# An RWKV time mixer and an MLP mixer on one core: PSUM banks by order of release, one product moved to ScalarE, one chunk in another style, and a new order of all tasks

## The chip, the cores and the metric

The kernel runs on one core of a Trainium2 chip. A core has five engines with a queue of their own each: TensorE (PE), which multiplies matrices, VectorE (DVE), ScalarE (ACT), GpSimd (POOL) and SyncE (SP), which here issues transfers. Each takes its instructions strictly in the order in which they were written and waits on semaphores for the others. TensorE writes its results to PSUM, a memory of eight banks, from which VectorE and ScalarE take them. Transfers between the chip's main memory (HBM) and the on-chip SBUF run on 16 DMA engines. The metric is the device time in microseconds (us).

## The reference

The inputs r, k and v are [4, 8, 768, 48] (batch, heads, steps, head size) in f32, w and u are [8, 48]. First comes a recurrence over the steps, with one 48x48 state for each batch and head:

```python
for t in range(S):
    cur = einsum('bhd,bhe->bhde', u[None] * kt, vt)
    y[:, :, t] = einsum('bhd,bhde->bhe', rt, state + cur)
    state = w[None, :, :, None] * state + einsum('bhd,bhe->bhde', kt, vt)
```

With the heads put side by side y is x, [4, 768, 384]. It goes through a mixer over the steps and one over the channels, with weights [768, 256], [256, 768], [384, 1536] and [1536, 384]:

```python
h = maximum(xt @ w_tok1, 0) @ w_tok2        # xt is x with steps and channels exchanged
u = x + h.transpose(0, 2, 1)
out = u + maximum(u @ w_ch1, 0) @ w_ch2
```

## The kernel before

**The recurrence by chunks.** The 768 steps of a batch are six chunks of 128; there are 24 units (batch b, chunk c), numbered n = 6b + c. `unit` (it starts at `n = b * C + c`) writes the tasks of one. Powers of the decay w are multiplied into k (`kp`, which lies with its r partner in one of four tiles `kr`) and into r; both are transposed so that the head size lies on the partitions (`rk`); `scores` multiplies them (TensorE, `at_ps`, two banks for the even and odd heads); `masked` multiplies that with a mask of earlier steps (VectorE, `AT`); `outputs` multiplies with v, adds the state's part (`y_ps`), and `result` adds the own step's part `yd` (`x_b`). `add_state` gathers k times v in a bank for three chunks (`kv_ps`), and `keep_state` copies it; at the end of three chunks it is multiplied with `wGm`, a decay mask, on VectorE. `copy_v` casts v to bf16 (`vb`, ScalarE), and `own` makes `yd` on GpSimd from `vb` and the per-head sums `adg`.

The list `style` says how a unit's r and k are turned and how its `adg` is made:

- 'f32': TensorE transposes r unscaled in f32 (`trr`) and k scaled (`trk`), VectorE multiplies the decay into r as it takes it (`evac_r`); GpSimd makes `m` = k times r, TensorE transposes it (`mT_ps`) and multiplies with u (`ad_ps`). Two copies on ScalarE (`copy_m`, `copy_ad`) and one of the keys (`evac_k`) belong to it.
- 'pe': GpSimd or VectorE scales both (`mul_k`, `mul_r`), TensorE transposes them in one go (`turn_all`, `tr_ps`), ScalarE copies (`evac`). For `adg` GpSimd makes `ku` (`mul_u`), VectorE `rku` (`mul_rku`) and a sum over each head (`sum_rku`).
- 'dma': as 'pe', but a transposing DMA that SP issues (`turn_rk`) makes `rk`.

**The mixers.** `mixer` writes the tasks of one batch: `hidden` and `relu_h` (token mixing, `h1_ps`, named h_ps in the profile), `back` and `sum_u` (`hT_ps`, `u_sb`), then u transposed in two halves sg of three chunks each, on TensorE for batch 0 (`turn_pe`, `t_ps`, `copy_uT`) and by DMA for the others; `up` and `relu_z` for each of the 12 blocks jt of 128 hidden channels (`z_ps`, `zr`), `down` in three parts of four matmuls for each chunk (`h2_ps`, also h_ps in the profile), `sum_o` (`osb`) and a store.

**The order.** Nothing here is scheduled as the kernel is built: `add` files each task under a number, and `plan.run(ORDER)` calls the tasks in the order of a long list of numbers at the head of the file. The costs, ranks, `take` and `give` in the calls of `add` are read by nothing in the file. The list fixes the order within each engine's queue, and thereby which tasks wait for each other; the semaphores come from the tiles. 33 of the tasks are `keep_warm` fillers, matmuls on zeros that nobody reads, placed in the list like the others; 12 more stand at the start.

**PSUM.** Four banks serve the five tiles of the recurrence's core. The other four are a pool, `psM`, with `bufs=4` and the tag "m": each new tile takes the bank after that of the tile before, in rotation, and has to wait until what was last in that bank has been read. All mixers' tiles, all transposes and the fillers go through it.

**Loads.** SP issues 72 loads of 128 x 384 f32, from rows of 48 numbers, each of them a task of its own, and the stores and transposing DMAs between them. The weights are five DMAs on GpSimd's queue (`load_weights`: w_tok1, w_tok2, two halves of w_ch1, w_ch2), with a cast from f32 to bf16 on the way; `W_DEP` ties the issue of the fourth to the landing of k of batch 1, chunk 1, and that of the fifth to k of batch 1, chunk 2.

Of the kernel before, what the change touches and what calls it, by code (L numbers as in the profile page):

```python
# [21 lines left out]
class Plan:  # L22
# [17 lines left out]
    69, 71, 70, 72, 73, 74, 153, 1, 76, 146, 156, 12, 147, 0, 158, 165, 75, 13, 157, 14, 170, 154, 2, 15,  # L40
    160, 78, 148, 171, 174, 175, 3, 167, 77, 161, 4, 169, 177, 179, 79, 162, 168, 186, 163, 178, 181, 80,
    191, 5, 172, 195, 196, 200, 192, 81, 188, 202, 164, 198, 149, 182, 216, 6, 82, 190, 199, 203, 24, 207,
    189, 23, 166, 83, 25, 204, 212, 219, 183, 205, 217, 173, 220, 85, 209, 228, 7, 193, 206, 84, 211, 224,
    221, 208, 237, 225, 184, 88, 238, 226, 223, 185, 86, 240, 213, 249, 242, 187, 210, 227, 87, 233, 241,
    245, 229, 244, 234, 230, 89, 194, 263, 141, 246, 231, 254, 214, 90, 259, 232, 247, 255, 215, 42, 251,
    258, 248, 265, 235, 270, 253, 266, 142, 29, 261, 236, 267, 30, 95, 35, 262, 250, 252, 268, 143, 272,
    269, 256, 274, 277, 20, 26, 16, 257, 31, 589, 273, 271, 279, 275, 590, 276, 27, 280, 591, 19, 283, 40,
    592, 34, 593, 150, 28, 32, 17, 610, 594, 611, 606, 614, 595, 612, 94, 8, 33, 613, 615, 598, 22, 607,
    151, 93, 18, 46, 599, 286, 608, 38, 602, 91, 609, 287, 600, 291, 295, 596, 601, 21, 144, 105, 292, 616,
    44, 9, 43, 603, 617, 297, 47, 96, 152, 41, 642, 322, 650, 597, 644, 643, 315, 651, 646, 10, 645, 604,  # L50
    145, 652, 647, 316, 605, 648, 319, 278, 653, 49, 618, 649, 628, 323, 619, 624, 629, 11, 313, 284, 625,
    626, 285, 640, 314, 636, 627, 92, 664, 641, 637, 638, 665, 634, 296, 298, 639, 288, 635, 632, 301, 289,
    662, 633, 620, 290, 663, 302, 621, 622, 303, 660, 656, 623, 630, 661, 657, 306, 97, 631, 320, 308, 293,
    321, 658, 307, 102, 654, 391, 294, 659, 671, 99, 655, 324, 331, 333, 672, 100, 325, 666, 304, 326, 103,
    305, 667, 334, 309, 332, 311, 98, 310, 668, 337, 312, 104, 673, 669, 349, 338, 674, 101, 327, 329, 339,
    350, 328, 354, 670, 330, 352, 107, 676, 370, 356, 353, 106, 342, 371, 340, 357, 343, 375, 358, 345, 344,
    341, 109, 382, 373, 359, 346, 377, 389, 111, 361, 347, 360, 363, 374, 348, 362, 366, 110, 677, 365, 367,
    678, 364, 108, 397, 378, 390, 392, 384, 675, 679, 379, 402, 368, 112, 386, 380, 403, 385, 396, 691, 425,
    369, 381, 692, 395, 414, 383, 114, 387, 693, 398, 388, 116, 406, 696, 694, 695, 426, 408, 117, 429, 681,
    113, 697, 407, 409, 698, 682, 423, 699, 115, 701, 412, 683, 700, 413, 448, 442, 703, 702, 399, 704, 706,  # L60
    424, 680, 401, 419, 705, 707, 420, 440, 684, 431, 686, 400, 430, 415, 436, 443, 687, 441, 437, 404, 685,
    708, 446, 688, 120, 432, 709, 453, 405, 416, 457, 447, 689, 710, 418, 449, 711, 713, 417, 459, 690, 723,
    714, 712, 721, 724, 719, 722, 727, 126, 720, 715, 728, 476, 733, 716, 731, 118, 734, 725, 732, 735, 726,
    127, 433, 736, 421, 435, 729, 121, 454, 474, 434, 717, 730, 737, 422, 119, 718, 450, 508, 738, 438, 124,
    451, 766, 458, 452, 749, 123, 439, 767, 750, 460, 464, 768, 509, 475, 455, 463, 771, 477, 125, 465, 747,
    481, 512, 466, 757, 748, 480, 470, 772, 456, 758, 471, 769, 491, 773, 122, 753, 489, 774, 770, 745, 492,
    754, 775, 741, 746, 490, 131, 467, 742, 495, 751, 497, 132, 469, 761, 506, 752, 468, 762, 498, 484, 129,
    472, 507, 482, 486, 743, 128, 485, 739, 483, 744, 502, 473, 763, 740, 513, 503, 487, 764, 755, 531, 488,
    130, 759, 542, 756, 791, 765, 760, 496, 523, 525, 514, 786, 133, 792, 793, 515, 519, 787, 520, 540, 135,
    796, 798, 797, 794, 524, 788, 799, 134, 795, 516, 789, 801, 800, 536, 517, 805, 803, 537, 776, 802, 790,  # L70
    541, 777, 543, 140, 778, 559, 547, 781, 518, 548, 546, 782, 779, 549, 783, 804, 138, 553, 526, 499, 806,
    780, 808, 529, 530, 814, 809, 784, 812, 815, 501, 818, 807, 582, 500, 824, 813, 819, 820, 825, 822, 136,
    821, 550, 823, 576, 810, 551, 826, 785, 811, 552, 830, 137, 827, 828, 831, 504, 139, 829, 816, 505, 557,
    533, 817, 521, 534, 532, 866, 554, 522, 867, 574, 560, 868, 558, 832, 535, 565, 834, 869, 833, 836, 564,
    563, 835, 575, 538, 577, 837, 570, 848, 571, 870, 566, 846, 539, 581, 849, 861, 580, 847, 862, 583, 863,
    555, 864, 567, 556, 838, 865, 569, 856, 839, 568, 857, 584, 572, 585, 858, 573, 852, 859, 840, 853, 586,
    860, 844, 841, 850, 845, 587, 851, 842, 588, 854, 843, 886, 855, 881, 888, 887, 882, 896, 900, 897, 898,
    883, 901, 899, 889, 871, 884, 902, 890, 891, 872, 892, 885, 873, 893, 874, 876, 894, 875, 877, 895, 878,
    927, 929, 879, 928, 949, 930, 880, 941, 950, 931, 942, 945, 932, 947, 946, 903, 948, 921, 904, 925, 922,
    911, 926, 905, 912, 923, 906, 915, 924, 919, 916, 917, 920, 907, 918, 909, 908, 913, 910, 943, 914, 939,  # L80
    944, 961, 940, 956, 957, 951, 952, 953, 958, 954, 937, 955, 959, 933, 938, 960, 935, 934, 962, 936, 963,
    966, 967, 964, 968, 965, 976, 969, 977, 970, 971, 978, 972, 973, 979, 980, 974, 975,
# [4 lines left out]
def kernel(  # L87
# [29 lines left out]
    WARM = 3  # L117
    TR = 1.28
    STORE = ["SP"] * B
    RK = 4  # L120
    style = ['f32', 'f32', 'f32', 'f32', 'f32', 'f32', 'pe', 'pe', 'pe', 'pe', 'f32', 'f32', 'dma', 'dma', 'dma', 'dma', 'dma', 'dma', 'dma', 'dma', 'dma', 'dma', 'dma', 'dma']
    TURN_PE = {(0, c) for c in range(C)}
    DVE_KP = (0, 1, 2, 4, 7, 9,)
    W_AT = (19.5, 21.5, 23.5, 0.0, 0.0)
# [10 lines left out]
    psM = ctx.enter_context(tc.tile_pool(name="psM", bufs=4, space=bass.MemoryType.PSUM))  # L135
# [50 lines left out]

    def keep_warm(n):
        for _ in range(n):
            z_ps = psM.tile([128, 512], f32, name="idle_ps", tag="m")
            pe.matmul(z_ps, warm[:, 0:128], warm, start=True, stop=True)  # L190

# [38 lines left out]
    wd_ps = psM.tile([128, H], f32, name="wd_ps", tag="m")  # L230
# [19 lines left out]
    def decay_rT(g):  # L250
        if g == 0:
            for a in range(HP):
                act.activation(wpT[:, g, a, :], steps[:, ts(g, T)], Exp, scale=lnwd[:, a:a + 1])
        else:
            act.activation(wpT[:, g], wpT[:, g], Exp)
# [6 lines left out]
    for q in range(2):  # L262
        rows = slice(q * P, (q + 1) * P)
        act.activation(lnwd[rows, :], wd_ps[rows, q::2], Ln)
    decay_rT(0)
# [40 lines left out]
    exps = {g: setup("POOL", 1.05, lambda g=g: exponents(g), (-1, g), after=6.3) for g in (1, 2)}  # L306
    t_wn = {g: setup("ACT", 0.52, lambda g=g: decay_k(g), (0, g, 0)) for g in (1, 2)}
    t_wpT = {g: setup("ACT", 0.53, lambda g=g: decay_rT(g), (0, g, 0), [exps[g]]) for g in (1, 2)}

    def group_decay():  # L310
# [3 lines left out]
    t_wGm = setup("POOL", YD, lambda: pool.tensor_mul(  # L314
        wGm, bm, wG.unsqueeze(2).unsqueeze(3).to_broadcast([128, HP, 2, D])), (1, 0), [t_wG])
# [16 lines left out]
    for i, (n, c) in enumerate(((48, 0.0574), (16, 0.152), (24, 0.152), (24, 0.152), (96, 0.081))):  # L332
        t_w[i] = add("POOL", 0.85, lambda i=i: load_weights(i), rank=(-2, i), late=1.2, dma=(n, c), after=W_AT[i], deps=[t_load.get(W_DEP.get(i))])

    u_ps = {}

    def turn_u():
        u_ps["d"] = psM.tile([128, 3], f32, name="ud_ps", tag="m")
        pe.matmul(u_ps["d"], u_rows, ident_f[0:3, 0:3], start=True, stop=True)

    def block_u():
        dve.tensor_mul(u_blk, heads, u_ps["d"].unsqueeze(2).to_broadcast([128, 3, H]))

    def spread_u():
        u_ps["b"] = psM.tile([128, dm], f32, name="u_ps", tag="m")
        pe.matmul(u_ps["b"], ones, u_row, start=True, stop=True)

    def copy_u():
        act.copy(u_bc, u_ps["b"])

# [21 lines left out]
    def unit(b, c, prev):  # L372
# [36 lines left out]
        def turn(key, src, idt, dt):  # L409
            def f():  # L410
                L[key] = psM.tile([128, HP, T], dt, name=key, tag="m")
                for a in range(HP):
                    pe.transpose(L[key][:, a, :], pair(src(), a), idt)
            return f
# [6 lines left out]
        def turn_m():  # L421
            L["mT_ps"] = psM.tile([128, 3, T], f32, name="mT_ps", tag="m")
# [339 lines left out]
```

## Time and profile before

The seven runs of the kernel have a median of 174.89 us, from 173.38 to 176.16.

| what | us |
|---|---|
| the profiled execution's own time | 174.34 |
| its span, first to last instruction | 172.6 |
| TensorE busy | 163.9 |
| of that, fillers (`idle_ps`) | 14.9 |
| VectorE, ScalarE, GpSimd busy | 110.0, 91.8, 88.9 |
| TensorE's last matmul starts | 168.9 |
| last load issued by SP | 119.9 |

The span is what the page's rows add up to; the 1.7 us between it and the execution's time lie outside the recorded instructions. In the page a row of 40 digits gives an engine's busy share, in tenths, in each fortieth of the span (4.3 us). A group row reads: line, engine, operation, what is written and from what, count, then busy time in all and nanoseconds of one, then the idle time ahead of these instructions and what ended it. Every line is L143, the helper that writes all instructions in program order, so the tiles' names tell the work apart. Rows in order of time give start, duration, engine, and in brackets an idle time and what ended it. TensorE's matmuls overlap in the pipeline, so that rows are longer than the distance of their starts: 0.49 us from one `up` task (three matmuls) to the next.

### The profile page before, as it was taken

How to read it: one execution, taken by the hardware profiler on the slowest of the kernel's cores; microseconds unless marked ns; L12 is line 12 of the kernel's file. 1: busy time of each engine (PE TensorE's matmuls, PEld its weight loads, DVE VectorE, ACT ScalarE, POOL GpSimd, SP SyncE). 2: the span in 40 equal slices, each digit the busy share in tenths (PEclk: the TensorE clock that was granted, in tenths of full speed). 3: DMA queues.
4: the chain of work that ended last, by engine and by line, in shares of the span. 5: the costliest groups of instructions: out<-in, count | busy, mean ns of one | idle time of the engine just before them, and what ended most of it. 6: DMA issues, size and time to landing. Idle time of an engine off the chain costs nothing.

```text
span 172.6 us, 3854 instructions
## 1 busy us (share of the span) xinstructions
PE 163.9 (95%) x1456; PEld 103.9 (60%) x1457; DVE 110.0 (64%) x197; ACT 91.8 (53%) x211; POOL 88.9 (51%) x108
## 2 busy tenths in 40 slices
PE   6999898999799999999999899999999999999992
PEld 2568785556466787656566466565666656566560
DVE  7577994868946979799289862993958154000321
ACT  2899560389798287131965574048552510992300
POOL 5459799079900977999844999514850000000000
PEclk9999999999999999999999999999999999999999
DMA  4999999999998599899999999999571108200222
GB/s 91 203 199 198 175 184 213 204 188 166 197 187 165 117 223 219 178 234 157 241 221 152 257 227 172 189 242 227 106 167 49 46 1 202 70 4 0 91 91 91
DMA packets 101722, 27.38 MB, mean 159 GB/s; under 512 B 95173, under 2 KB 101705, under 8 KB 101705
## 3 DMA queue, kind: packets, MB, share of 16 engines
q1 hardware_dynamic: 98112, 23.80, 73.6%
q0 software_dynamic: 3408, 3.15, 11.4%
q10 hardware_dynamic: 184, 0.20, 0.5%
q8 instruction: 11, 0.18, 0.4%
q14 instruction: 7, 0.05, 0.1%
HBM read 20.65 MB, written 4.72 MB: 147 GB/s over the span
## 4 chain that ended last, share of the span: by engine, by line
PE 54%; DMA 19%; SPq 11%; DVE 9%; POOL 2%; issue 2%; ACT 0%; POOLq 0%; DVEq 0%
PE h_ps L143 24%; PE z_ps L143 19%; SPq L143 11%; DMA kt<-in_k_dram 8%; DMA wch<-in_moe_w_ch_dram 5%; DMA wtok<-in_moe_w_tok_dram 4%; DVE u_sb L143 3%; PE y_ps L143 3%; PE hT_ps L143 3%; PE at_ps L143 2%; DVE rku L143 2%; DVE AT L143 2%; DMA vt<-in_v_dram 2%; POOL ku L143 1%; POOL yd L143 1%
## 5 line engine op out<-in xcount | busy, mean ns | idle before, releaser
L143 ACT ACTIVATE zr<-z_ps 128x384 bf16<-128x384 f32 x96 | 45.5, 493 | 30.8 <-PE z_ps L143 30.5
L143 PE MATMUL z_ps<-uT,wch 128*128 128x384 bf16 x288 | 51.1, 326 | 1.2 <-DMA wch<-in_moe_w_ch_dram 1.2
L143 PE MATMUL h_ps<-wch,zr 128*128 128x384 bf16 x288 | 52.2, 326 | 0.0
L143 DVE TENSOR_TENSOR AT<-at_ps,mask 128x512 bf16<-128x512 f32 x48 | 31.5, 684 | 13.2 <-PE at_ps L143 13.2
L143 PEld LDWEIGHTS <-wch 128*128 128x128 bf16 x288 | 27.0, 98 | 19.0 <-DMA wch<-in_moe_w_ch_dram 1.5
L143 PEld LDWEIGHTS <-zr 128*128 128x128 bf16 x288 | 27.3, 98 | 16.8
L143 POOL TENSOR_TENSOR yd<-vb,adg 128x384 f32<-128x384 bf16 x24 | 20.8, 868 | 21.2 <-ACT vb L143 9.9
L143 DVE TENSOR_TENSOR osb<-u_sb,h_ps 128x384 f32<-128x384 bf16 x24 | 13.2, 550 | 24.4 <-PE h_ps L143 24.3
L143 DVE TENSOR_TENSOR rku<-ku,rt 128x384 f32<-128x384 f32 x16 | 19.9, 1248 | 2.7 <-POOL ku L143 2.4
L143 POOL TENSOR_TENSOR ku<-kt,u_bc 128x384 f32<-128x384 f32 x16 | 16.7, 1050 | 7.5 <-DMA kt<-in_k_dram 7.4
L143 POOL TENSOR_TENSOR kr<-kt,wn 128x384 bf16<-128x384 f32 x18 | 18.7, 1037 | 0.0
L143 POOL TENSOR_TENSOR kr<-rt,wp 128x384 bf16<-128x384 f32 x16 | 16.9, 1058 | 3.4 <-DMA rt<-in_r_dram 3.3
L143 DVE TENSOR_TENSOR u_sb<-x_b,hT_ps 128x384 bf16<-128x384 bf16 x24 | 12.3, 545 | 9.1 <-PE hT_ps L143 9.1
L143 ACT CAST vb<-vt 128x384 bf16<-128x384 f32 x24 | 12.3, 511 | 10.6 <-DMA vt<-in_v_dram 10.4
L143 DVE TENSOR_TENSOR x_b<-y_ps,yd 128x384 bf16<-128x384 f32 x24 | 13.2, 551 | 5.9 <-PE y_ps L143 5.0
L143 PE MATMUL idle_ps<-warm 128*128 128x512 bf16 x44 | 14.9, 432 | 1.7 <-DVE warm L143 1.5
L143 PEld LDWEIGHTS <-rk 48*128 48x128 bf16 (+1 forms) x272 | 10.2, 95 | 7.9 <-issue 5.6
L143 ACT CAST S<-kv_ps 48x192 bf16<-48x192 f32 x32 | 10.0, 312 | 6.7 <-PE kv_ps L143 5.2
L143 PEld LDWEIGHTS <-wtok 128*128 128x128 bf16 x96 | 8.8, 98 | 7.3 <-DMA wtok<-in_moe_w_tok_dram 1.2
L143 PEld LDWEIGHTS <-kr 128*128 128x128 bf16 x144 | 9.3, 99 | 3.8 <-issue 0.9
L143 PE MATMUL hT_ps<-h1r,wtok 128*128 128x384 bf16 x48 | 10.3, 326 | 0.1
L143 POOL TENSOR_TENSOR m<-kt,rpad 128x384 f32<-128x384 f32 x8 | 8.5, 1066 | 2.9 <-PE kv_ps L143 1.8
(72 smaller groups left out, 159.0 us busy)
## 6 DMA issues: line engine op xcount, KB each, us to landing
kt<-in_k_dram SPq DMA_DIRECT2D x24, 192.0 KB, 4.1
vt<-in_v_dram SPq DMA_DIRECT2D x24, 192.0 KB, 4.3
out_dram<-osb SPq DMA_DIRECT2D x24, 192.0 KB, 2.6
rt<-in_r_dram SPq DMA_DIRECT2D x16, 192.0 KB, 3.8
rpad<-in_r_dram SPq DMA_DIRECT2D x8, 192.0 KB, 4.6
wch<-in_moe_w_ch_dram POOLq DMA_DIRECT2D x2, 576.0 KB, 9.0
wch<-in_moe_w_ch_dram POOLq DMA_DIRECT2D x1, 1152.0 KB, 13.9
wtok<-in_moe_w_tok_dram POOLq DMA_DIRECT2D x2, 384.0 KB, 7.1
```

The lines of the kernel that those rows point to most:

```text
L143: return lambda *args, **kw: tc.keep_in_program_order(f(*args, **kw))
```

## The change

Four things change in the code; the list `ORDER` is replaced.

1. PSUM banks: a small class hands out the four banks of `psM` from a list of free ones. A tile takes the bank that has been free longest; the task that reads the tile last gives the bank back at that place of the program. Each bank has a tag of its own with one buffer.
2. `wGm` is made by four ScalarE activations with a per-partition scale, no longer by one GpSimd product. (The tuple `EXPS` names the groups whose decay GpSimd prepares; it holds the same two groups as before.)
3. Unit 10 (batch 1, chunk 4) goes from style 'f32' to 'pe'. It has three tasks less, so the tasks' numbers after it shift.
4. The planning numbers of the weights change, which nothing in the file reads.

```diff
+    class Buffers:
+        def __init__(self, pool, tag, n):
+            self.pool, self.tag, self.free, self.held = pool, tag, list(range(n)), {}
+
+        def take(self, shape, dtype, name):
+            i = self.free.pop(0)
+            t = self.pool.tile(shape, dtype, name=name, tag=f"{self.tag}{i}", bufs=1)
+            self.held[id(t)] = (i, t)
+            return t
+
+        def give(self, t):
+            self.free.append(self.held.pop(id(t))[0])
+
+    banks = Buffers(psM, "m", 4)
...
-                L[key] = psM.tile([128, HP, T], dt, name=key, tag="m")
+                L[key] = banks.take([128, HP, T], dt, key)
...
             def evac_k():
                 act.copy(rk_tile()[:, 0], L["trk"])
+                banks.give(L["trk"])
...
-    t_wGm = setup("POOL", YD, lambda: pool.tensor_mul(
-        wGm, bm, wG.unsqueeze(2).unsqueeze(3).to_broadcast([128, HP, 2, D])), (1, 0), [t_wG])
+    def group_mask():
+        for a in range(HP):
+            act.activation(wGm[:, a], bm[:, a], ACTF.Copy, scale=wG[:, a:a + 1])
+
+    t_wGm = setup("ACT", 0.75, group_mask, (1, 0), [t_wG])
...
-    style = [... 'pe', 'pe', 'pe', 'pe', 'f32', 'f32', 'dma', ...]
+    style = [... 'pe', 'pe', 'pe', 'pe', 'pe', 'f32', 'dma', ...]
```

All other tiles of `psM` are taken and given back in the same manner. Of the new order, this is what the prediction speaks of. The number of fillers is the same. On GpSimd, w_tok1 is issued behind five `m`, one `kp` and two `yd` (before: five `m`, one `kp`, four `yd` and `wGm`), and between the fourth and fifth weights stand `ku`, `kp`, `yd`, `ku`, `mul_r` (before: two `ku`). On SP, v of batch 0, chunk 2 is the 16th issue (before: the 10th), r of batch 0, chunk 1 the 9th (before: the 5th), and r and k of batch 1, chunk 4 the 28th and 27th (before: the 33rd and 32nd). On ScalarE the cast of v of batch 1, chunk 0 stands ahead of the first mixer's relu (before: behind it and the first `copy_uT`). On TensorE the units of batches 1 to 3 stand ahead of more of the mixers' `up` and `down` tasks than before, and nine fillers lie between the last `hidden` of batch 0 and its first `up` (before: 16). On VectorE `rku` of batch 1, chunk 4 and that of chunk 2 stand ahead of the first `masked` of batch 1, and that of chunk 3 stands between the masks of chunks 0 and 1.

## Prediction

> **What bounds the kernel now.** I read the page's busy rows first, then the same rows by stage, then TensorE's own instructions in order of time, then the queues that feed it.
>
> ```profile
> PE 163.9 (95%) x1456; PEld 103.9 (60%) x1457; DVE 110.0 (64%) x197; ACT 91.8 (53%) x211; POOL 88.9 (51%) x108
> PE   6999898999799999999999899999999999999992
> ...
> PEclk9999999999999999999999999999999999999999
> ...
> L143 PE MATMUL idle_ps<-warm 128*128 128x512 bf16 x44 | 14.9, 432 | 1.7 <-DVE warm L143 1.5
> ```
>
> TensorE is busy nearly everywhere at full clock, but 14.9 us of that are fillers (`idle_ps`) that compute nothing. The stages, cut at the first channel-mixing matmul (`z_ps`), show where they lie:
>
> ```profile
> 0.00:38.60 38.60, 35.62 (x331) 23.29 (x333) 28.41 (x64) 22.75 (x58) 25.76 (x44) 1.00 1.08 184
> 38.60:45.60 7.00, 5.87 (x43) 3.55 (x41) 5.94 (x4) 6.62 (x15) 6.98 (x8) 1.00 1.13 180
> 45.60:130.00 84.40, 83.22 (x818) 53.50 (x819) 63.99 (x109) 46.48 (x106) 56.15 (x58) 1.00 1.06 192
> ```
>
> Before 38.60 TensorE waits for loads, units and weights and fills the time; after it, it works almost without a hole. In order of time:
>
> ```profile
> 37.72 1.04 PE L143 MATMUL idle_ps<-warm 128*128 128x512 bf16 x3
> 38.60 2.11 PE L143 MATMUL z_ps<-uT,wch 128*128 128x384 bf16 x12
> ...
> 45.63 0.66 PE L143 MATMUL z_ps<-uT,wch 128*128 128x384 bf16 x3 [1.16 <-DMA wch<-in_moe_w_ch_dram]
> ```
>
> Two holes more of this kind follow: 0.68 us before `kv_ps` at 77.96 and 0.47 us before `at_ps` at 99.23. So the span is the time of the first `z_ps` (38.6), the work behind it, 2.3 us of holes, and 3.4 us from TensorE's last matmul (169.2) to the end (one VectorE sum, 0.56, and a store). Whatever shortens the span must bring the first `z_ps` forward, take work from TensorE, or close holes; whatever opens new holes behind 38.6 costs its full length.
>
> **The change, part by part.** *Banks.* No instruction is added or removed. Where TensorE waited for a bank in this profile is read from the waits: 0.5 us (`mT_ps` for the copy of `adg`), 0.5 (`at_ps`, which the change doesn't touch) and 0.3 (weights for `zr`). So the new hand-out is worth between 0 and 0.8 us by itself; I take 0, because each bank is still waited for by the task that takes it, and the rest of its worth is in what order it allows.
>
> *Mask product to ScalarE.* GpSimd loses one `wGm` product, 0.83 us at 16.6, which stands ahead of the token weights' issue. ScalarE gets four products of 128x96. Near rows are the 48x192 cast, 312 ns, and the 128x8 copy, 164 ns, so 4 x 164 = 0.65 to 4 x 312 = 1.25 us. They stand behind the key copy of chunk 2; behind them wait `copy_ad` of chunk 2 and `copy_m` of chunk 1. ScalarE has 2.4 us of idle time between 16.4 and 20.0 (0.60, 0.47 and 1.33 us before three of its rows), so I cost it at 0; without that cover it would be up to 1.25 us on the first `z_ps`.
>
> *Chunk 10 (batch 1, chunk 4) as 'pe' in place of 'f32'.* From the chain of the last work, TensorE loses `trr` 0.44, `trk` 0.22, `mT_ps` 0.48 and `ad_ps` 0.62, and gains one `tr_ps` of eight transposes, 0.45: 1.3 us less. ScalarE swaps 0.59 + 0.49 + 0.16 for one copy of 1.01 us. GpSimd does `kr`, `kr`, `ku` for `kr`, `m`: 1.0 us more. VectorE swaps one `rk` product (0.68) for `rku` (0.84 in the middle of its rows) and a sum (0.55): 0.7 us more. GpSimd and VectorE have the room on average, not in every stretch (below).
>
> *The order, the front.* Before, GpSimd issues `wtok1` at 21.80, behind five m products, a kr product, four yd, the wGm and the two exponents. After, two yd and wGm stand behind the issue or are gone: 3 x 0.83 = 2.5 us less ahead of it, of which I take 2.0, since the m product of chunk 1 now waits for a load that is issued ninth and not fifth. So `wtok1` is issued at 19.8 and lands at 26.6 with the 6.8 us that it took. The value load of chunk 2 moves from the tenth to the sixteenth place in SP's queue, where this trace issues at 16.0 and loads land some 5 us later, at 21.0; its state and the work that is written behind it up to the first token matmul (4.4 us of TensorE) put that at 26.6 too, against 28.62. This gain is then eaten: behind it stand four fillers and the last chunk's output, whose mask product waits in VectorE's queue for a `rku` of the next batch. I get the last token matmul at 31.0 (30.86 before). From there to the first `z_ps` it is 7.7 us before, with 16 fillers; after, there are nine, sg0 comes first in place of sg1, and all six `t_ps` stand ahead. Six VectorE sums at 0.46 apart, the last behind one kr product, end at 36.6; the last transpose follows, two fillers, and `z_ps` starts at 37.3: 1.3 us earlier. The bounds are 36.3 (as the fillers count) and 38.6 (as before). The TensorE tasks ahead of it are also 0.3 us more, taken from behind.
>
> *The order, the weights.* They are GpSimd's own issues.
>
> ```profile
> 35.66 1.12 POOL L143 TENSOR_TENSOR yd<-vb,adg 128x384 f32<-128x384 bf16 x1 [5.79 <-DVE u_sb L143]
> 36.73 0.80 POOL L143 DMA_DIRECT2D wch<-in_moe_w_ch_dram  x1
> 37.55 1.97 POOL L143 TENSOR_TENSOR ku<-kt,u_bc 128x384 f32<-128x384 f32 x2
> 39.45 1.07 POOL L143 DMA_DIRECT2D wch<-in_moe_w_ch_dram  x1
> ```
>
> The second half of w_ch1 waits 5.79 us behind a yd; that is the 1.16 us hole at 45.63. The VectorE work named was done at 31.9; its last input is the cast `vb` on ScalarE, at 35.03, behind a `copy_uT`. After, this cast stands ahead of the mixer's first relu in ScalarE's queue, and the next limit is the key load of batch 1, chunk 1, which the issue is tied to: with loads landing some 2.8 us apart while weights move, about 33.5, and the issue at 34.5. With 8.85 us it lands at 43.4; its first use is at 43.1, so this hole closes, within what the estimate can tell. w_ch2 moves back: five GpSimd products stand between the two issues in place of two, and I get its issue at 42 for 39.45, since `ku` of chunk 4 waits for its key. Its 13.9 us shared the queue with the piece before (landed 7.8 us apart), so alone I estimate 10.5 to 13.9, landing 52.5 to 56; the first down matmul stands at 52.8 unstalled and 55 with the holes below. I take no hole, up to 1.5.
>
> *The order, the units behind.* TensorE's list asks for everything earlier. Counting its rows from 37.3, the mask inputs (`at_ps`) of batch 1, chunk 4 stand at 54.7 (before 64.55), the next batch's token matmuls at 63 (70.66), batch 2, chunk 4 at 87 (96.46), batch 3, chunk 5 at 122 (131.25). SP's queue at its present pace allows that: the last r/k turn is its 99th issue, and the 98th of this trace is at 119.9 with some 4 us of pauses. The narrow place is batch 1. The r load of chunk 4 lands near 42 by the loads moved, so its `rku` runs to 43.5; the next `rku`, two sums and two mask products (0.68 each) follow in VectorE's order, and the masks of chunk 0 end at 47.6 where TensorE wants the next `at_ps` at 46.3. A further `rku` does the same once more, 0.7. I take 2.0 us of holes there, and 1.15 later, as the two of this trace.
>
> Sum against the profiled execution (span 172.6, its time 174.34): -1.3 (chunk 10), -0.3, -1.3 (first `z_ps`), -2.3 (old holes), +3.2 (new ones) = -2.0, span 170.6. That execution lies 0.55 below the median of 174.89, so 174.9 - 2.0 = 172.9.
>
> **A rule against it.** `rku` has a row far off its group:
>
> ```profile
> 40.35 0.55 DVE L143 TENSOR_REDUCE adg<-rku 128x8 f32<-128x384 f32 x1
> 40.90 0.27 DVE L143 MEMSET kr<- 128x256 uint32 x1
> 41.09 6.43 DVE L143 TENSOR_TENSOR rku<-ku,rt 128x384 f32<-128x384 f32 x1
> ```
>
> GpSimd runs products back to back from 40.55 to 47.1, and `rku` ends 0.4 us behind them. The Trainium skill (SBUF — State Buffer, section "SBUF: two separate sides") says that a VectorE instruction with two SBUF inputs and a GpSimd one exclude each other for one whole instruction. By the rule as it reads, `rku` waits for one product, 1.0 us, and the holes stay at 3.2; by this row it waits for the whole run. It speaks against this change, which puts `rku` ahead of masks that TensorE waits for. Nine of 16 `rku` took under 0.9 us, six 0.95 to 1.35, so I hold to the short ones and make the long one a rival.
>
> **The rivals.** *The order holds (170.9).* If the batch-1 holes don't come, the sum has 1.15 in place of 3.2: -4.05. For it: the new holes rest on a landing that I estimate to within 2 us. Against: VectorE's queue has no slack there.
> *Weights late (174.4).* w_ch2 lands as late as it did after its issue: 1.5 us more, -0.5. For it: 13.9 is the row; against: it shared its queue.
> *VectorE shut out (176.7).* In batch 1, between 42 and 55, `rku` of chunks 4 and 3 wait to the end of GpSimd's runs of three to four products (45.0 and 52.1, when GpSimd itself comes to a product that needs their sums). The masks of chunk 0 and 1 then end at 48.6 and 55.0, where TensorE wants them at 46.5 and 49.9: 5.1 us of holes, 1.15 later and 0.8 for one more such case: 7.05 for 3.2, +1.8. From 5.2 us of holes on nothing is gained; from 6.9 it is over 1% slower.
>
> **How the numbers follow.** Chances: sum as worked 0.33, order holds 0.25, weights late 0.18, shut out 0.24. A measurement of this kernel tells about 1% (1.75 us) from no change. Below 173.1 lie the order case, over half of the likeliest and little of the late weights: 0.46. Above 176.6 lies some two thirds of the shut-out case and a tail of the others: 0.21. The rest, 0.33, is within 1%. The predicted time is the likeliest, 172.9 (its own range 171.5 to 174.3); the range of all runs from 170.4 to 177.4.
>
> **What would show it.** Right: first `z_ps` near 37.3 with fewer fillers just ahead; no wait on `wch` over 0.5 us at 43 to 45; holes on TensorE of about 2 us between 44 and 55, behind `AT`; `rku` under 1.4 us. Wrong: first `z_ps` at 38.6 or later (a yd, a load or a bank ahead of it), holes over 5 us behind the first `z_ps` (`AT`, `wch`, `kr`), or none at all.

## The result, and the profile after

The changed kernel takes 173.49 us (median of 24 runs), the kernel before 174.54 us in the runs that were taken with it (61 in all). The ratio is 0.9918, with a 95% interval from 0.9892 to 0.9943: 0.8% faster, about 1.4 us. Some executions of every kernel are disturbed, longer and mostly at a lower granted clock; all ratios and median spans below leave them out, and without them the changed kernel's median is 172.90. The profiled execution took 173.01 us, with a span of 171.0 (172.6 before).

The busy rows, the groups of the fillers and of `rku`, and the shares of the chain of work that ended last, from the page of the changed kernel:

```profile
PE 163.5 (96%) x1447; PEld 104.0 (61%) x1448; DVE 106.6 (62%) x198; ACT 91.1 (53%) x213; POOL 89.7 (52%) x108
...
PEclk9999999999999999999999999999999999999999
DMA  4999999999999999999999999899421146100222
...
PE 77%; DMA 12%; DVE 6%; ACT 1%; issue 1%; SPq 1%; ACTq 0%; DVEq 0%
...
L144 DVE TENSOR_TENSOR rku<-ku,rt 128x384 f32<-128x384 f32 x17 | 16.4, 963 | 3.1 <-POOL ku L144 2.0
L144 PE MATMUL idle_ps<-warm 128*128 128x512 bf16 x44 | 16.0, 452 | 1.6 <-DVE warm L144 1.5
```

TensorE is on the chain for 77% of the span (54% before), yet it still spends 16.0 us on fillers (14.9 before, of the same number). What it won was not won ahead of the first `z_ps`. The stages and TensorE's rows from there on:

```profile
0.00:38.86 38.86, 36.47 (x338) 24.62 (x340) 28.33 (x65) 24.73 (x65) 26.44 (x44) 1.00 1.10 181
38.86:45.60 6.74, 6.03 (x44) 3.69 (x43) 3.17 (x7) 5.26 (x14) 5.19 (x6) 1.00 1.05 203
45.60:130.00 84.40, 83.39 (x828) 53.11 (x826) 65.24 (x110) 47.58 (x108) 58.04 (x60) 1.00 0.99 190
```

```profile
38.86 2.11 PE L144 MATMUL z_ps<-uT,wch 128*128 128x384 bf16 x12
41.62 0.33 PE L144 MATMUL kv_ps<-vb,kr 128*128 128x96 bf16 x4 [0.65 <-ACT vb L144]
...
53.71 0.40 PE L144 MATMUL at_ps<-rk 48*128 48x128 bf16 x8 [1.01 <-DVE AT L144]
```

The first `z_ps` stands at 38.86, not earlier than the 38.60 before. Behind it there are two holes, 1.66 us in all, both in batch 1; the three of before (2.31 us) are gone, the wait for `wch` among them. The span divides as follows:

| us | before | after | difference |
|---|---|---|---|
| first `z_ps` | 38.60 | 38.86 | +0.26 |
| holes behind it | 2.31 | 1.66 | -0.65 |
| the rest behind it | 131.69 | 130.48 | -1.21 |
| span | 172.6 | 171.0 | -1.6 |

### The profile page after: what moved, and what is told of

Read it like the earlier page. It is cut to its first block, busy times and chain, and to the rows that moved or that the text cites. A ratio compares the mean times of both kernels' runs of the same rounds, so it can differ in the third digit from the quotient of the medians.

```text
span 171.0 us, 3824 instructions
## 1 busy us (share of the span) xinstructions
PE 163.5 (96%) x1447; PEld 104.0 (61%) x1448; DVE 106.6 (62%) x198; ACT 91.1 (53%) x213; POOL 89.7 (52%) x108
## 4 chain that ended last, share of the span: by engine, by line
PE 77%; DMA 12%; DVE 6%; ACT 1%; issue 1%; SPq 1%; ACTq 0%; DVEq 0%
PE h_ps L144 31%; PE z_ps L144 22%; DMA vt<-in_v_dram 6%; DMA rt<-in_r_dram 4%; PE y_ps L144 4%; PE at_ps L144 4%; PE hT_ps L144 4%; PE idle_ps L144 3%; DVE rku L144 2%; DMA wp<-in_w_dram 2%; PE trr L144 2%; PE kv_ps L144 2%; PE ad_ps L144 2%; DVE AT L144 1%; PE mT_ps L144 1%; DVE kr L144 1%
## 5 line engine op out<-in xcount | busy, mean ns | idle before, releaser
L144 PE MATMUL z_ps<-uT,wch 128*128 128x384 bf16 x288 | 52.0, 326 | 0.1
L144 PE MATMUL h_ps<-wch,zr 128*128 128x384 bf16 x288 | 51.6, 326 | 0.0
L144 PEld LDWEIGHTS <-wch 128*128 128x128 bf16 x288 | 26.6, 98 | 16.7 <-issue 0.2
L144 POOL TENSOR_TENSOR kr<-kt,wn 128x384 bf16<-128x384 f32 x18 | 19.5, 1085 | 3.2 <-DMA kt<-in_k_dram 1.4
L144 POOL TENSOR_TENSOR ku<-kt,u_bc 128x384 f32<-128x384 f32 x17 | 17.6, 1036 | 5.4 <-DMA kt<-in_k_dram 4.8
L144 POOL TENSOR_TENSOR kr<-rt,wp 128x384 bf16<-128x384 f32 x17 | 17.9, 1054 | 2.5 <-DMA rt<-in_r_dram 2.5
L144 DVE TENSOR_TENSOR rku<-ku,rt 128x384 f32<-128x384 f32 x17 | 16.4, 963 | 3.1 <-POOL ku L144 2.0
L144 PE MATMUL idle_ps<-warm 128*128 128x512 bf16 x44 | 16.0, 452 | 1.6 <-DVE warm L144 1.5
L144 PEld LDWEIGHTS <-kr 128*128 128x128 bf16 x148 | 10.1, 99 | 4.5 <-issue 1.4
L144 PE MATMUL at_ps<-rk 48*128 48x128 bf16 x192 | 9.6, 218 | 1.0 <-DVE AT L144 1.0
L144 PE MATMUL hT_ps<-h1r,wtok 128*128 128x384 bf16 x48 | 9.4, 326 | 0.1
```

Source lines behind the costliest of these rows:

```text
L144: return lambda *args, **kw: tc.keep_in_program_order(f(*args, **kw))
```

## The experiments

Ratios are to the kernel before on the same chip, with 95% intervals.

### The changed kernel once more

No edit.

> The changed kernel again, nothing edited, for a second trace. Two theories for its first up matmul (z_ps) at 38.86 us where 37.3 was predicted. Chance: TensorE's half pace up to 10.2 us in the first trace was one execution's; here transposes and fillers run at full pace from about 6 us, first scores stand at 10 to 11 us, z_ps near 37.4, span near 169.6. Order: the list itself makes it late (the last chunk's masks stand behind a rku and a sum of the next batch, and the first z_ps behind five sums): z_ps again at 38.5 to 39.2 and span 170.5 to 171.5, wherever the pace turns. Ratio to the kernel before 0.990 to 0.994 by either.

Measured: 172.24 us in the profile, ratio 0.9893 (0.9801 to 0.9985). TensorE's start was fast. Its rows, of the first trace and then of this one:

```profile
6.28 1.46 PE L144 MATMUL idle_ps<-warm 128*128 128x512 bf16 x3
```

```profile
6.11 0.82 PE L144 MATMUL idle_ps<-warm 128*128 128x512 bf16 x3
```

The same three fillers take 0.82 us in place of 1.46, and the `at_ps` of 19.57 in the first trace stands at 17.68 here. But that lead of 1.9 us is lost at once, in a wait for an `m` of GpSimd that the first trace does not have; the next `at_ps` stands at 22.32 for 22.61:

```profile
20.82 0.55 PE L144 MATMUL mT_ps<-ident_f,m 128*128 128x128 f32 x3 [1.43 <-POOL m L144]
```

So the first `z_ps` follows at 38.45: the two starts differ by 0.4 us there, and the other 1.15 to the predicted 37.3 are in the order or in the loads. The holes behind it are 1.58 us, though not the same ones:

```profile
44.14 0.40 PE L144 MATMUL tr_ps<-ident,kr 128*128 128x128 bf16 x4 [0.74 <-POOL kr L144]
53.02 0.40 PE L144 MATMUL at_ps<-rk 48*128 48x128 bf16 x8 [0.84 <-DVE AT L144]
```

The first hole waits here for GpSimd's scaled r of batch 1, chunk 0, which stands behind a `ku` that waited 2.13 us for k of chunk 4, and there for v of chunk 2: around 42 us TensorE runs into the loads, whichever comes last. The second recurs.

### Chunk 10 alone

```diff
-    style = [... 'pe', 'pe', 'pe', 'pe', 'f32', 'f32', 'dma', ...]
+    style = [... 'pe', 'pe', 'pe', 'pe', 'pe', 'f32', 'dma', ...]
```

in the kernel before; in its list 350 (`m`) becomes `mul_r`, `mul_u`, 352 (`trk`) becomes `turn_all`, 353 (`evac_k`) becomes `evac`, 356 (`evac_r`) becomes `mul_rku`, `sum_rku`, and the chunk's other 'f32' tasks go.

> The kernel before with chunk 10 (batch 1, chunk 4) alone turned to 'pe': banks in rotation, wGm on GpSimd, old list, the new tasks in the places of the old ones (mul_r and ku where m stood, rku and its sum where evac_r stood, the one turn where trk stood). The prediction's term: TensorE 1.3 us less work behind the first z_ps, so 173.0 for 174.3, ratio 0.9925. Rival: the two more GpSimd products (1.0 us) and the rku and sum (0.7 us on VectorE) come late in a list not made for them, and TensorE waits as much as it saves: ratio 0.998 to 1.004, with a new wait on kr, AT or tr_ps of 1 us or more between 55 and 70 us.

Measured: ratio 1.0019 (0.9969 to 1.0068); median span 172.7, that of the kernel before on this chip 172.7. The 1.3 us (0.9925) did not arrive. TensorE's rows of the stretch, then VectorE's:

```profile
63.62 0.33 PE L141 MATMUL y_ps<-S,rk 128*128 128x96 bf16 x4
64.06 0.20 PE L141 MATMUL y_ps<-vb,AT 128*128 128x48 bf16 x1
64.66 0.35 PE L141 MATMUL y_ps<-vb,AT 128*128 128x48 bf16 x7 [0.40 <-DVE AT L141]
64.94 0.40 PE L141 MATMUL at_ps<-rk 48*128 48x128 bf16 x8
```

```profile
61.88 0.93 DVE L141 TENSOR_TENSOR rku<-ku,rt 128x384 f32<-128x384 f32 x1
62.85 0.55 DVE L141 TENSOR_REDUCE adg<-rku 128x8 f32<-128x384 f32 x1
63.33 1.28 DVE L141 TENSOR_TENSOR AT<-at_ps,mask 128x512 bf16<-128x512 f32 x2
```

From the first `y_ps` row to the next `at_ps` it is 1.32 us; in the kernel before the same tasks take 0.46 (64.09 to 64.55). VectorE's new `rku` and sum stand ahead of the masks that these outputs wait for, and 0.86 us of the 1.3 go back at once. What is left is too little to be seen in the time; in this one trace the part behind the first `z_ps` is, without its holes, 131.05 us for 131.69. So what TensorE saved counted here only for what the list did not make it wait for VectorE again.

### Banks in rotation

```diff
-            i = self.free.pop(0)
-            t = self.pool.tile(shape, dtype, name=name, tag=f"{self.tag}{i}", bufs=1)
+            i = 0
+            t = self.pool.tile(shape, dtype, name=name, tag=self.tag)
...
-            self.free.append(self.held.pop(id(t))[0])
+            pass
```

with `bufs=4` for `psM` again; all else as changed.

> The changed kernel with its four banks again handed out in rotation; list, style and wGm stay as changed. The prediction costs the hand-out by itself at 0 (0 to 0.8): ratio to the kernel before within 0.003 of the changed kernel's (0.992), 173.0 to 173.8. Rival: the new list leans on banks that come free out of turn (its hidden banks and down banks are held long while z_ps pass), so in rotation tiles wait for them: 2 to 6 us slower than the changed kernel, waits of z_ps, t_ps or idle_ps for ScalarE's or VectorE's reading of unrelated tiles.

Measured: ratio 0.9968 (0.9925 to 1.0012), median span 171.9. The next kernel, on the same chip and with the hand-out kept, has 170.85. The intervals overlap, so that the size, about 1 us, is not settled. The trace names two waits that no trace with the hand-out has, those of `z_ps` and `t_ps`:

```profile
PE at_ps L144 <- DVE AT L144: 1.0, 1, 1.0
PE z_ps L144 <- DVE osb L144: 0.9, 1, 0.9
...
PE t_ps L144 <- ACT uT L144: 0.4, 1, 0.4
```

This is the table of TensorE's waits (us in total, times, longest). A `z_ps` needs nothing of `osb`; it waits for its bank, which VectorE has yet to read. The same holds for `t_ps` and the copy `uT`. By the rival (2 to 6 us) the list would have fallen apart in rotation; it did not.

### wGm on GpSimd again

```diff
-    def group_mask():
-        for a in range(HP):
-            act.activation(wGm[:, a], bm[:, a], ACTF.Copy, scale=wG[:, a:a + 1])
-
-    t_wGm = setup("ACT", 0.75, group_mask, (1, 0), [t_wG])
+    t_wGm = setup("POOL", YD, lambda: pool.tensor_mul(
+        wGm, bm, wG.unsqueeze(2).unsqueeze(3).to_broadcast([128, HP, 2, D])), (1, 0), [t_wG])
```

> The changed kernel with wGm made by one GpSimd product again, at the same place of the list (between the mask product of chunk 0 and the m product of chunk 3 or next to it). The prediction costs the move at 0: ScalarE's four take 1.5 us, beside idle time. If 0: same time within 0.3 us. Rival: GpSimd's 0.83 us stand ahead of w_tok1's issue (20.79), so it lands at 28.1 for 27.3, hidden(0,1,2) waits for it (27.9 before) and all up to the first z_ps moves by up to 0.8: +0.2 to +0.8 us.

Measured: ratio 0.9919 (0.9878 to 0.9960), as the changed kernel's. GpSimd's rows show why:

```profile
13.56 1.00 POOL L144 TENSOR_TENSOR m<-kt,rpad 128x384 f32<-128x384 f32 x1 [2.33 <-DVE rk L144]
14.52 0.83 POOL L144 TENSOR_TENSOR wGm<-bm,wG 128x384 f32<-128x384 f32 x1
...
19.24 1.00 POOL L144 TENSOR_TENSOR m<-kt,rpad 128x384 f32<-128x384 f32 x1 [0.39 <-PE y_ps L144]
20.18 1.00 POOL L144 DMA_DIRECT2D wtok<-in_moe_w_tok_dram  x1
```

With the product back in its queue GpSimd still waits 0.39 us ahead of the `m` in front of w_tok1's issue, and issues it at 20.18; the changed kernel issues it at 20.79 and 20.71. The product did not hold that issue up.

### The kernel before once more

No edit.

> The kernel before again, nothing edited, for a second trace. The first traces differ at the start: four early fp32 transposes took 0.60 us in the kernel before and 1.06 in the kernel with chunk 10 alone, whose first z_ps stands 1.8 us later though its list up to there is the same. Theory: TensorE's pace up to 10 us is one or the other in each execution of any kernel, and the old list passes it on. If this trace starts fast (three fillers near 6 us take 0.8 to 0.93): z_ps at 38.4 to 38.8, span 171.5 to 172.8. If it starts slowly (1.46): z_ps at 40 to 40.6, span 173.2 to 173.8. Rival: the start doesn't set z_ps (38.6 in either).

Measured: 177.53 us in the one execution, too far from the other times of this kernel to compare. Its start was fast (0.82 us for the three fillers) and its first `z_ps` nevertheless at 41.46, behind a wait of 2.04 us for w_tok1: a fast start alone does not bring the `z_ps` early. One row is of use below: the long `rku` is there again, 6.42 us.

### One GpSimd product less beside rku

Task 314 is `mul_r` of batch 1, chunk 2, and 323 the `yd` of that chunk:

```diff
-    296, 649, 113, 285, 629, 316, 314, 659, 102, 650, 319, 302, 630, 288, 660, 323, 635,
+    296, 649, 113, 285, 629, 316, 659, 102, 650, 319, 302, 630, 288, 660, 323, 314, 635,
```

> The changed kernel with the mul_r product of batch 1, chunk 2 moved on GpSimd behind the yd of the same chunk, so that one product and not two runs while rku of that chunk waits. If rku waits for GpSimd's whole run: 2.2 to 2.4 us fall to 1.2 to 1.4, the masks of chunk 0 end 1.0 us earlier. If it waits for one product only (the 1.22 of the second trace), it stays as it falls, 1.2 to 2.4, whatever GpSimd runs behind. On the time: 0 to -0.4, since the hole before at_ps of chunk 2 was 0.84 us also where rku took 1.22.

The rows of `rku` of that chunk and of GpSimd beside it, in the changed kernel's first trace, in its second, and here:

```profile
43.85 1.07 POOL L144 DMA_DIRECT2D wch<-in_moe_w_ch_dram  x1
44.92 2.40 DVE L144 TENSOR_TENSOR rku<-ku,rt 128x384 f32<-128x384 f32 x1
44.94 1.96 POOL L144 TENSOR_TENSOR kr<-rt,wp 128x384 bf16<-128x384 f32 x2
```

```profile
44.02 1.07 POOL L144 DMA_DIRECT2D wch<-in_moe_w_ch_dram  x1
45.15 2.26 POOL L144 TENSOR_TENSOR kr<-rt,wp 128x384 bf16<-128x384 f32 x2
45.33 1.22 DVE L144 TENSOR_TENSOR rku<-ku,rt 128x384 f32<-128x384 f32 x1
```

```profile
44.33 1.01 POOL L142 TENSOR_TENSOR kr<-rt,wp 128x384 bf16<-128x384 f32 x1
44.70 1.07 DVE L142 TENSOR_TENSOR rku<-ku,rt 128x384 f32<-128x384 f32 x1 [0.30 <-DMA rt<-in_r_dram]
...
46.27 1.28 DVE L142 TENSOR_TENSOR AT<-at_ps,mask 128x512 bf16<-128x512 f32 x2
```

Beside this pair `rku` waits out both products (2.40; 2.39 and 2.22 in two other kernels); in the second trace it got in between them, and GpSimd's pair grew from 1.96 to 2.26. Beside one it takes 1.07, and the masks of chunk 0 start at 46.27 for 47.83 and 47.06. The time does not follow: 0.9926 (0.9882 to 0.9969). The hole before the `at_ps` of chunk 2 is even longer in this trace, since the next `rku` (chunk 3) now waits 0.89 us for its `ku`, which the moved product has pushed back:

```profile
49.60 1.34 DVE L142 TENSOR_TENSOR rku<-ku,rt 128x384 f32<-128x384 f32 x1 [0.89 <-POOL ku L142]
...
53.12 0.40 PE L142 MATMUL at_ps<-rk 48*128 48x128 bf16 x8 [1.65 <-DVE AT L142]
```

### The next rku behind the masks

Tasks 334 and 337, `rku` of batch 1, chunk 3 and its sum, go behind 294, the first `result` of batch 1:

```diff
-    306, 634, 334, 293, 332, 627, 308, 320, 628, 337, 631, 349, 321, 294, 657,
+    306, 634, 293, 332, 627, 308, 320, 628, 631, 349, 321, 294, 334, 337, 657,
```

> The changed kernel with rku of batch 1, chunk 3 and its sum moved on VectorE from between the masks of chunks 0 and 1 to behind the first result of batch 1. The hole before the at_ps of chunk 2 (1.01, 0.84 and 1.00 us in the traces so far) is put down to this rku (1.35 us, beside a GpSimd product) standing ahead of the second mask of chunk 1. If so: the hole goes or falls under 0.2, span 0.8 to 1.0 shorter, 172.1 to 172.4. Rival: the masks' place is taken by the next wait (masks of chunk 2 behind the moved rku, or the first down matmul, which has 1.5 us on the landing of w_ch2): the same 1 us of holes before at_ps of chunk 3 or h_ps, time within 0.3.

Inconclusive: only one of its four times can be compared, 172.98 us, which neither shows the gain of 1 us nor excludes it.

### The way to the first z_ps cleared

The head of the edit (280, 283: `rku` and sum of batch 1, chunk 0; 256: outputs of chunk 4; 268: `ad_ps` of chunk 5; 586, 587, 588: the token matmuls; 589, 590: the relus; 286: the cast):

```diff
-    272, 280, 267, 586, 143, 270, 273, 277, 268, 283, 91, 274, 256, 269, ...
+    272, 267, 256, 268, 586, 143, 270, 273, 277, 91, 274, 269, ...
...
-    286, 275, 93, 587, 287, 276, 291, 150, 19, 588, 292, 29, 20, 590, 21, 589, 31, 27, ...
+    275, 93, 587, 276, 150, 19, 588, 589, 286, 590, 29, 20, 21, ...
...
-    610, 612, 597, 606, 309, 315, ...
+    610, 612, 280, 283, 606, 315, 287, ...
```

Behind 286 goes 291, the state of that chunk. Four fillers are left out, and further back w_ch2 and some `up` tasks move forward.

> The changed kernel with the way to the first z_ps cleared: rku and sum of batch 1, chunk 0 off VectorE's queue ahead of the last masks of batch 0 (behind the six sums), outputs of chunk 4 and ad_ps of chunk 5 ahead of the first token matmuls, the casts of v of batch 1 behind the mixer's relus, t_ps of chunk 1 first, four fillers less, w_ch2 issued ahead of ku of batch 1, chunk 4, and the ups of the first half of w_ch1 ahead of the first turn of batch 1. Theory: these waits, not the start, hold the first z_ps at 38.4 to 38.9; it comes to 35.5 to 36.5, and 1 to 2 us of that stay in the span: 171.0 to 172.0. Rival: from 38 to 55 us the loads and w_ch2 set the pace (DMA engines 99% busy); what is won ahead of z_ps comes back as holes on kr, at_ps or wch, time within 0.5 of the changed kernel or later.

Measured: ratio 1.0019 (0.9963 to 1.0075), 1% slower than the changed kernel; first `z_ps` at 39.15. The `rku` is out of the way, and so is the state of batch 1, chunk 0, and TensorE waits all the same. Its rows, then GpSimd's:

```profile
26.01 0.63 PE L142 MATMUL trr<-ident_f,rpad 128*128 128x128 f32 x4 [1.48 <-DMA rpad<-in_r_dram]
...
33.69 0.48 PE L142 MATMUL h_ps<-x_b,wtok 128*128 128x384 bf16 x2 [1.03 <-DVE x_b L142]
```

```profile
25.94 1.00 POOL L142 TENSOR_TENSOR m<-kt,rpad 128x384 f32<-128x384 f32 x1 [2.09 <-DMA rpad<-in_r_dram]
28.70 0.99 POOL L142 TENSOR_TENSOR ku<-kt,u_bc 128x384 f32<-128x384 f32 x1 [1.76 <-DMA kt<-in_k_dram]
29.65 0.83 POOL L142 TENSOR_TENSOR yd<-vb,adg 128x384 f32<-128x384 bf16 x1
```

The last `x_b` waits for its `yd`, and the `yd` stand in GpSimd's queue behind `m` and `ku`, which wait for loads. Most of the loss lies further back: of the 2.5 us between this span (173.5) and that of the changed kernel's first trace 0.3 stand ahead of the `z_ps`, 1.4 are holes behind it (3.07 us, 1.65 of them before the `at_ps` of chunk 2), and 0.8 are not accounted for. Two things were not tried: to take `ku` out of that queue, and to turn chunk 10 back to 'f32' in the new list.

## Why the prediction was right, and where it was not

The time was predicted as 172.9 and measured as 173.49, with a profile of 173.01. The total is right in part by luck: the first `z_ps` came 1.56 us later than worked, and the holes behind it were 1.54 us shorter. The two hang together in part. The first place where holes were foreseen, the second `at_ps` of batch 1, has none, since TensorE comes to it at 49.12 and not at 46.3, just as the masks end (49.11, for 47.6).

**The first `z_ps` (-1.3): wrong.** It came to 38.86 and 38.45; the first of these is one of the prediction's own signs of being wrong (38.6 or later). The steps that failed are the state of chunk 2 and what is written behind it, which "put that at 26.6 too", and "I get the last token matmul at 31.0". The first and last token matmul were at 27.89 and 32.69; from there on it took 6.17 us to the `z_ps`, as worked (6.3). w_tok1 was issued at 20.79 for 19.8 and landed at 27.29 for 26.6. The slow start explains about 0.4 us. One wait was overlooked: TensorE's list has the state of batch 1, chunk 0 ahead of the last token matmul, and its cast `vb` waited 1.88 us for v, which landed at 31.72, 9.6 us after its issue:

```profile
32.31 0.33 PE L144 MATMUL kv_ps<-vb,kr 128*128 128x96 bf16 x4 [0.28 <-ACT vb L144]
32.48 0.38 PE L144 MATMUL idle_ps<-warm 128*128 128x512 bf16 x1
32.69 0.49 PE L144 MATMUL h_ps<-x_b,wtok 128*128 128x384 bf16 x2
```

The last `x_b` was there at 32.04, so this is worth at most 0.65 us; the `rku` ahead of the masks (1.17 us at 27.50) is another holder. Neither was the only one, as the run that moved both shows: there a `yd` comes next, behind loads. From the issue the prediction subtracted 2.5 us of products and took 2.0; it got 1.0. GpSimd stands idle between its products (2.19 and 1.39 us ahead of the issue in the first trace, 2.32 and 1.50 in the second), so that what one product leaves is filled by waiting. That the waits are for loads is argued: the rows name another engine in each trace, and in the run with the front cleared a load of r (2.13).

**Chunk 10 and the rest behind the first `z_ps` (-1.3 and -0.3): right within 0.4.** Without holes that part is 1.21 us shorter (1.4 in the second trace). That this is chunk 10's work is argued from the count of TensorE's tasks; no run took it out of the new list. The cover that the prediction only asserted "on average" matters: with the old list the same edit shows no gain in time.

**The old holes (-2.3): right.** All three are gone. The fourth weights were issued at 34.06 (34.5) and landed at 40.07 (43.4), the fifth at 43.85 (42) and 55.47 (52.5 to 56), ahead of the first `down` matmul at 56.99: no hole, as taken. The rival of late weights falls.

**The new holes (+3.2): mis-sized, 1.66 measured.** The place is right for 1.0 of them, the `at_ps` of batch 1 behind `AT` at 53; the other 0.65 wait for a load at 42, and the 1.15 of "later" did not come. That the masks' hole comes from the `rku` of chunk 3 is argued from the order of the rows: the run that moved it left it open, and the one that brought the masks of chunk 0 forward to 46.27 did not bring the second mask of chunk 1 forward, in front of which that `rku` stands (52.39; 52.98 and 52.29 in the two traces of the changed kernel).

**The banks (0, bounds 0 to 0.8): probably mis-sized.** In rotation the median span is some 1 us longer, with 0.9 and 0.4 us of waits for banks in view. The bound came from the bank waits of the old order; the new order makes its own.

**wGm (0): right**, but for GpSimd's idle time as much as for ScalarE's: its four products took 1.19 us, near the upper bound.

**The rule weighed against the trace.** Both readings occurred. Of the 17 `rku` of the first trace one, that of chunk 2, waited out GpSimd's products (2.40 us); no other took more than 1.35. The "VectorE shut out" rival had those of chunks 4 and 3 wait to the end of GpSimd's rows of products. That of chunk 4 came late, by its r load, and took 0.56. That of chunk 3 stood beside a row of four products without a gap, from 48.85 to 53.35, and got in:

```profile
48.85 1.00 POOL L144 TENSOR_TENSOR ku<-kt,u_bc 128x384 f32<-128x384 f32 x1
49.80 1.31 POOL L144 TENSOR_TENSOR kr<-rt,wp 128x384 bf16<-128x384 f32 x1
50.18 1.35 DVE L144 TENSOR_TENSOR rku<-ku,rt 128x384 f32<-128x384 f32 x1
```

It ended at 51.53, 0.41 us behind the product beside which it had started, as the rule reads. The rival needs 5.2 us of holes to give back the gain, and there were 1.66. "The order holds" missed by less: 1.15 us of holes asked for, with a `z_ps` that did not come.

So -2.0 was made of -1.3, -0.3, -1.3, -2.3 and +3.2; what came is +0.3 at the `z_ps`, -1.2 in the work and -0.65 in the holes.

## What to carry to other kernels

A gain "ahead of the path" that is worked out by subtracting instructions from a queue needs the idle time in that queue: where an engine waits for loads between its instructions, a shorter list waits longer. An instruction saved on the bound engine counts in full only if what replaces it elsewhere does not stand ahead of that engine's next input. And waits for banks read from the old order need not bound what a new order will need.

## What the runs showed of the hardware

TensorE's first microseconds have two paces. Three fillers near 6 us take 0.82 us or 1.46, eight fp32 transposes at 7 to 9 us 1.04 or 1.79, from one execution to the next of the same kernel, and the slow pace lasts to about 10 us. The clock row shows 9 throughout in both. The Trainium skill (TensorE: Matmul & The Clock Gate, section "Part 1: The HAM clock gate (the "warmup" mystery)") says that the turn to full rate depends on a free-running window and so varies between runs, by 500 ns either way. That it varies is so here; but it varies by some 4 us, and only the durations show it.

A VectorE product of two SBUF inputs and GpSimd's products wait for each other, in two manners. In the ten traces of all runs 94 `rku` stand beside a GpSimd product that another followed at once. Of these, 86 ended 0.41 or 0.42 us behind the product beside which they had started, and GpSimd's next one grew (the `kr` from 1.00 us to 1.31 in the median). The other eight were held to the end of all the products in the row: 6.42 or 6.43 us in three traces with the old list, 2.08 to 2.40 beside a pair. All eight stand beside a row of products whose first began 0.02 us behind GpSimd's issue of weights, as at 44.94 above. In two traces the first product began 0.06 us behind such an issue (45.15 above is one), and there `rku` got in. This was read from the traces afterwards; no run varied it, and the reason is open.
